# Load chunk sizes, fillers and the weights' gate, first weight products in halves of 256 columns, and output products moved into the first and split in the last block of an attention-and-MLP kernel

## The chip, the cores and the metric

The kernel runs on one core of one Trainium2 chip. The metric is the device time of one execution in microseconds (us). Beside it stands the span that the profiler records, from the first to the last instruction of one execution; it is some 1.8 us shorter. The mean granted TensorE clock of a run is 1.000, 0.999 or 0.998, and in traces with 0.998 there is one stretch of 3.4 us at half clock (0.5 x 3.41 / 756 = 0.0023). I call a run at 0.998 "clock lost". In traces at 0.999 half of that or less lies inside the span, and it comes after PE's last product, where it costs nothing; I count all runs at 0.999 as "clock kept".

The engines: PE multiplies (its weight loads are PEld), DVE is VectorE, ACT is ScalarE, POOL is GpSimd, SP issues DMAs.

## The reference

```python
# q, k, v: (4, 6080, 256); w_in (256, 2048); w_out (2048, 256)
qn = q / (norm(q, axis=1) + 1e-6);  kn = k / (norm(k, axis=1) + 1e-6)
s = kn.transpose(0, 2, 1) @ qn / tau          # 256 x 256 for each of 4 heads
a = softmax(s)
x = (v @ a).reshape(24320, 256)
out = gelu_tanh(x @ w_in) @ w_out
```

The contraction of `s` runs over all 6080 rows, so no output row can begin before all of q and k of its head is there.

## The kernel before

The kernel folds `a @ w_in` into one 256 x 2048 matrix `aw` for each head. A head's rows are then taken in blocks of 512. One block is 8 slots (`NP`); a slot is four hidden products `hp` of 512 columns (0.86 us), one Gelu of 1024 columns on ScalarE (1.02 us), and 8 of the 64 output products `yp` of the block before. Heads 1 to 3 do their attention in between. Only head 0's attention is exposed: the first 38 us load q and k in ten chunks and form the Gram matrix `G` and the column sums behind them. `keep_clock` issues products whose results nobody reads ("fillers"), so that PE's clock isn't lowered while PE waits for loads.

```python
    first_chunks = chunks_of([6, 6, 6, 6, 6, 6, 4, 3, 2, 2], 7)   # slots of 128 rows; 64 odd rows go with chunk 7
    fillers = [0, 0, 5, 5, 5, 5, 3, 2, 1, 0]
    ...
    for n, ch in enumerate(first_chunks):
        ...                                    # cast on DVE (L242), squares on ACT
        keep_clock(fillers[n])                 # L137
        for s, rows in slots_of(ch):
            gram(G, qkb, s, rows, ...)         # L141
        ...                                    # column sums, L153
        if n == n_chunks - 4:                  # the "gate": chunk 6 has landed
            nc.gpsimd.tensor_copy(gate[:, 0:1], st[0:1, 1, 0, 0:1])
    ...
    # GpSimd's DMA queue, in order, behind the gate:
    #   w_in in 4 parts, v of block 1, w_out in 2 halves, q/k of head 1 chunk 0, v of block 2
```

Then the softmax and the first part of `aw`:

```python
    nc.scalar.activation(r, cols[:, 0:4], AF.Sqrt)          # L320: starts when the last column sum is there
    norms(r); Gs = scaled(G, r); keep_clock(5); T = turned(Gs)
    ...                                                     # exponentials
    vT0 = ...; vps = ...                                    # 8 transposes of v block 0 on PE
    nc.scalar.activation(vT0, vps, AF.Copy)
    keep_clock(1)
    ...                                                     # ScalarE loads the Gelu table
    rsinv = row_sums(eT)
    ...
    ps0 = [aw_product(0, ic, pY, "y") for ic in range(2)]   # 4 products of 512 columns
    for lo in (0, 256):
        for ic in range(2):
            nc.vector.tensor_scalar_mul(aw[:, ic, lo : lo + 256], ps0[ic][:, lo : lo + 256], rsinv[:, ic : ic + 1])
    for ic in range(2):
        aw_part(eT, rsinv, aw, 1, ic)
    ...
```

The blocks, and the end:

```python
            for i in range(NP):
                ...                                         # hp, Gelu
                more_aw(1)
                if before is not None:
                    todo = [(s, fc) for s in range(len(before["rows"])) for fc in range(FC)]
                    for s, fc in todo[len(todo) * i // NP : len(todo) * (i + 1) // NP]:
                        y_part(before, s, fc, fc + 1)
    ...
    for s in range(4):                                      # the last block's own output
        y_part(before, s, 0, FC)
```

v of block n + 2 is turned by DMA transposes (SP, L294) from rows that GpSimd's queue fetched (L280).

## Time and profile before

| | before |
|---|---|
| time, median of 4 runs | 758.18 us (757.82 to 758.25) |
| span and clock of the profiled run | 756.4 us, 0.998 |
| last column sum ready (square root, L320, starts) | 38.27 us |
| from there to the start of the last group of hidden products | 705.33 us |
| from there to the end of the span | 12.79 us |

The last three rows add up to the span (38.27 + 705.33 + 12.79 = 756.39; the page rounds spans to 0.1, so ends are taken from the times in ns that the traces hold). I use this division into **front, middle and end**, because a timed median here moves by several tenths of a us, and a trace resolves hundredths.

The page's first part (busy us, share of the span, instructions) says that PE is the bound:

```profile
PE 738.3 (98%) x5248; PEld 504.5 (67%) x5248; DVE 278.2 (37%) x484; ACT 419.8 (56%) x411; POOL 70.7 (9%) x127
```

Of 756.4 us PE is idle for 18: 9.0 before its first product, 4.0 after its last, and 5.1 between, 4.6 of these while q and k load.

The chain in order of time (start, duration, what) has one more place that the change addresses, the only wait inside the blocks:

```profile
51.61 1.03 ACT g L540
...
52.68 1.02 PE hp L536 x4
```

PE waits there for a Gelu at the end of block 0, where it has no output products yet to do meanwhile.

### The profile page before, as it was taken

Reading aid. Unit: us, or ns where it says so; the run is one execution under the profiler, and the core shown is the slowest. Engines: PE = TensorE matmul, PEld = TensorE weight load, DVE = VectorE, ACT = ScalarE, POOL = GpSimd, SP = SyncE. Lnnn points to the kernel's source line nnn. Section 1 sums busy time; section 2 is a strip of 40 time slices with the busy share of each in tenths; the row PEclk is TensorE's granted clock in tenths of the full one; section 3 lists DMA queues with packets and bytes.
Section 4 is the critical chain, followed back from the end, with each engine's and each line's share of the span. In section 5 each row is a group of like instructions: output and inputs, shape, how many; then the busy total and the mean of one; then the engine's idle time right before and its main releaser. Section 6 shows DMA issues by size and latency. Waiting matters only on the chain.

```text
span 756.4 us, 12305 instructions
## 1 busy us (share of the span) xinstructions
PE 738.3 (98%) x5248; PEld 504.5 (67%) x5248; DVE 278.2 (37%) x484; ACT 419.8 (56%) x411; POOL 70.7 (9%) x127
## 2 busy tenths in 40 slices
PE   4899999999999999999999999999999999999997
PEld 3556666667666666666666666666767666666666
DVE  4644545454402555553421455454441011011011
ACT  5675555555465555555555555555546655555552
POOL 0321011001021011001031000100101000000000
PEclk9999999999999999999999999999999999999999
DMA  8999957225149778313549375621412633322111
GB/s 364 355 206 168 177 84 155 54 42 83 42 93 215 134 137 132 73 43 64 102 93 220 83 135 96 126 79 47 82 42 79 110 83 72 68 76 52 41 57 56
DMA packets 80599, 83.59 MB, mean 111 GB/s; under 512 B 55456, under 2 KB 60064, under 8 KB 80544
## 3 DMA queue, kind: packets, MB, share of 16 engines
q0 software_dynamic: 17648, 32.97, 26.5%
q1 hardware_dynamic: 62672, 48.98, 24.3%
q8 instruction: 41, 0.67, 0.4%
q10 hardware_dynamic: 224, 0.85, 0.3%
q14 instruction: 14, 0.11, 0.1%
HBM read 78.91 MB, written 24.90 MB: 137 GB/s over the span
## 4 chain that ended last, share of the span: by engine, by line
PE 95%; DMA 3%; ACT 1%; DVE 0%; SPq 0%; issue 0%; DVEq 0%; ACTq 0%
PE yp L463 44%; PE hp L536 43%; PE G L141 5%; DMA st<-in_k_dram 3%; PE ps L201 2%; PE cols L153 1%; ACT sqb L247 0%; PE idle L137 0%; PE T L179 0%; DVE qkb L242 0%; SPq L80 0%; ACT g L540 0%; PE ps L345 0%; PE vps L333 0%; DVE Gs L171 0%
## 5 line engine op out<-in xcount | busy, mean ns | idle before, releaser
L540 ACT ACTIVATE g<-hp 128x1024 bf16<-128x1024 f32 (+1 forms) x384 | 389.3, 1014 | 308.9 <-PE hp L536 308.9
L463 PE MATMUL yp<-wout_bf,g 128*128 128x256 bf16 x3040 | 393.3, 273 | 0.0
L536 PE MATMUL hp<-vT,aw 128*128 128x512 bf16 (+1 forms) x1536 | 390.5, 377 | 0.2 <-ACT g L540 0.2
L463 PEld LDWEIGHTS <-g 128*128 128x128 bf16 x3040 | 297.5, 98 | 112.9
L536 PEld LDWEIGHTS <-aw 128*128 128x128 bf16 x1536 | 150.0, 98 | 105.3 <-issue 1.1
L480 DVE COPY ysb<-yp 128x512 f32<-128x512 f32 (+1 forms) x95 | 64.9, 683 | 403.1 <-PE yp L463 395.1
L404 DVE TENSOR_TENSOR acc<-acc,sq 128x512 f32<-128x512 f32 (+1 forms) x141 | 97.6, 692 | 4.8
L141 PE MATMUL G<-qkb 128*128 128x256 bf16 (+1 forms) x384 | 70.7, 285 | 13.6 <-DVE qkb L242 13.6
L403 DVE TENSOR_TENSOR sq<-qkb 128x512 bf16<-128x512 bf16 (+1 forms) x141 | 58.9, 418 | 0.0
L141 PEld LDWEIGHTS <-qkb 128*128 128x128 bf16 (+1 forms) x384 | 38.2, 102 | 23.0 <-DVE qkb L242 15.6
L280 POOL DMA_DIRECT2D vb<-in_v_dram x47 | 25.5, 544 | 142.8 <-DMA vT<-vb 135.9
L210 DVE TENSOR_SCALAR aw<-ps,rsinv 128x512 bf16<-128x512 f32 x30 | 22.3, 750 | 25.6 <-PE ps L201 25.3
L80 POOL DMA_DIRECT2D qkb<-in_q_dram x24 | 13.0, 540 | 152.1 <-PE hp L536 83.0
L247 ACT ACTIVATE sqb<-st 128x3072 bf16<-128x3072 f32 (+3 forms) x9 | 20.4, 2286 | 11.2 <-DMA st<-in_k_dram 11.2
L242 DVE CAST qkb<-st 128x3072 bf16<-128x3072 f32 (+4 forms) x11 | 14.7, 1345 | 14.9 <-DMA st<-in_k_dram 14.9
L201 PE MATMUL ps<-win_bf,eT 128*128 128x512 bf16 x60 | 17.7, 379 | 0.0
L414 POOL TENSOR_TENSOR r<-r,half 128x4 f32<-128x4 f32 x3 | 3.1, 1041 | 141.5 <-DVE r L413 141.5
L80 POOL DMA_DIRECT2D qkb<-in_k_dram x24 | 13.1, 544 | 5.0 <-DMA qkb<-in_q_dram 2.2
L521 POOL COPY g<-gr 128x1024 bf16<-128x1024 bf16 x2 | 2.1, 1037 | 104.1 <-PE yp L463 104.1
L439 DVE RECIPROCAL den<-den 128x256 f32<-128x256 f32 x6 | 10.5, 1753 | 0.2
L549 POOL COPY gr<-g 128x1024 bf16<-128x1024 bf16 x2 | 2.1, 1034 | 87.6 <-ACT g L540 87.6
L137 PE MATMUL idle<-filler 128*128 128x512 bf16 x32 | 9.2, 408 | 0.0
(60 smaller groups left out, 81.0 us busy)
## 6 DMA issues: line engine op xcount, KB each, us to landing
out_dram<-ysb SPq DMA_DIRECT2D x44, 512.0 KB, 2.9
vb<-in_v_dram POOLq DMA_DIRECT2D x43, 256.0 KB, 8.5
qkb<-in_q_dram POOLq DMA_DIRECT2D x21, 384.0 KB, 6.2
qkb<-in_k_dram POOLq DMA_DIRECT2D x21, 384.0 KB, 8.3
st<-in_q_dram SPq DMA_DIRECT2D x6, 768.0 KB, 10.3
st<-in_k_dram SPq DMA_DIRECT2D x5, 768.0 KB, 11.8
vT<-vb SPq DMA_TRANSPOSE x184, 3.8
out_dram<-ysb SPq DMA_DIRECT2D x4, 384.0 KB, 4.2
```

Source lines behind the costliest of these rows:

```text
L80: engines[x].dma_start(out=dst[:, x, 0:size, :], in_=src[b, s0 * 128 : (s0 + size) * 128, :].rearrange("(p s) c -> p s c", s=size))
L141: nc.tensor.matmul(G[:, ic, :], lhsT=qk[:rows, 1, s, ic * 128 : ic * 128 + 128], rhs=qk[:rows, 0, s, :], start=first and ic == 0, stop=las ...
L201: nc.tensor.matmul(ps, lhsT=eT[:, jc, ic * 128 : ic * 128 + 128], rhs=win_bf[:, jc, fs * 512 : fs * 512 + 512], start=jc == 0, stop=jc == 1)
L210: nc.vector.tensor_scalar_mul(dst, ps, scale)
L247: nc.scalar.activation(sqb[:rows, :, lo:hi], st[:rows, :, lo:hi], AF.Square)
L280: nc.gpsimd.dma_start(out=t[:, 0:n, :], in_=v_rows[r0 : r0 + n * 128, :].rearrange("(p s) c -> p s c", s=n))
L403: nc.vector.tensor_mul(sq[:rows], flat, flat)
L404: nc.vector.tensor_add(acc[:rows], acc[:rows], sq[:rows])
L463: nc.tensor.matmul(yp[:rows, at, :], lhsT=g[:, fc, s * 128 : s * 128 + rows], rhs=wout_bf[:, fc, :], start=fc == 0, stop=fc == FC - 1)
L480: nc.vector.tensor_copy(ysb[:, s0 : s + 1, :], yp[:, 0 : s + 1 - s0, :])
L536: nc.tensor.matmul(hp[:, j, :cols], lhsT=aw[:, cc, fc * 128 : fc * 128 + 128], rhs=vT[:, cc, :cols], start=cc == 0, stop=cc == 1)
L540: nc.scalar.activation(g[:, 2 * i : 2 * i + 2, :cols], hp[:, :, :cols], AF.Gelu_apprx_tanh)
```

## The change

Four parts, all small against the span:

1. **Loads.** Other chunk sizes; the 64 odd rows come with chunk 2 instead of 7; three more fillers ahead of chunks 4 and 5, two more later; the weights' gate opens on chunk 7 instead of 6.
2. **Softmax to first hidden product.** T's transposes in an order that lets two of them start on half of `Gs`; v block 0 evacuated half by DVE, half by ACT; the filler ahead of the row sums gone; the first products of `aw` only 256 columns wide, so that the first hidden product needs less. The Gelu table is loaded after the first scalings.
3. **Block 0** does 12 of its own output products in its last three slots; block 1 then has 7 or 6 a slot instead of 8.
4. **The end.** The last slot's output in two halves of 128 columns, each with its own copy and transfer.

```diff
-    first_chunks = chunks_of([6, 6, 6, 6, 6, 6, 4, 3, 2, 2], 7)
+    first_chunks = chunks_of([6, 6, 5, 6, 6, 6, 4, 4, 2, 2], 2)
-    fillers = [0, 0, 5, 5, 5, 5, 3, 2, 1, 0]
+    fillers = [0, 0, 5, 5, 6, 7, 4, 3, 1, 0]
...
-        if n == n_chunks - 4:
+        if n == n_chunks - 3:
...
-        for jc in range(2):
-            for ic in range(2):
+        for ic in range(2):
+            for jc in range(2):
                 nc.tensor.matmul(T[:, jc, ...], ...)
...
-    nc.scalar.activation(vT0, vps, AF.Copy)
-    keep_clock(1)
+        if cc == 0:
+            nc.vector.tensor_copy(vT0[:, cc, :], vps)
+        else:
+            nc.scalar.activation(vT0[:, cc, :], vps, AF.Copy)
...
-    ps0 = [aw_product(0, ic, pY, "y") for ic in range(2)]
-    for lo in (0, 256): ...                   # four scalings on DVE
+    for lo, pool, tag in ((0, pY, "y"), (256, pA, "a")):
+        for ic in range(2):
+            ...                               # two products of 256 columns
+            if lo == 0 and ic == 1:
+                nc.scalar.activation(dst, ps[:, 0:256], AF.Copy, scale=scale)
+            else:
+                nc.vector.tensor_scalar_mul(dst, ps[:, 0:256], scale)
...
-                more_aw(1)
+                more_aw(2 if i == 0 else 1)
                 if before is not None:
+                    n = -(-len(before["todo"]) // (NP - i))
+                elif i >= NP - 3:
+                    n = 4
...
-    for s in range(4):
-        y_part(before, s, 0, FC)
+    ...                                       # slots 0 to 2 as before
+    for c0 in (0, 128):
+        ...                                   # 16 products of 128 columns
+        nc.vector.tensor_copy(ysb, yp)
+        for (lo, row), eng in zip(before["rests"], (nc.sync, nc.scalar)):
+            eng.dma_start(out=out[row : row + rest, c0 : c0 + 128], in_=ysb[lo : lo + rest])
```

More of the change, by code (lines that the diff above doesn't have):

```diff
@@ L329 @@
     vT0 = vts.tile([128, 2, 512], BF16, tag="vT", name="vT")
-    vps = pH.tile([128, 2, 512], FP32, tag="h", name="vps")
     for cc in range(2):
+        vps = pH.tile([128, 2, 512], FP32, tag="h", name="vps")[:, 0, :]
         for s in range(4):
-            nc.tensor.matmul(vps[:, cc, s * 128 : s * 128 + 128],
+            nc.tensor.matmul(vps[:, s * 128 : s * 128 + 128],
                              lhsT=v0[:, s, cc * 128 : cc * 128 + 128],
                              rhs=ident, is_transpose=True)
-    nc.scalar.activation(vT0, vps, AF.Copy)
@@ L337 @@
-    keep_clock(1)
-    nc.scalar.activation(dummy, ones_f, AF.Gelu_apprx_tanh)
+        if cc == 0:
+            nc.vector.tensor_copy(vT0[:, cc, :], vps)
+        else:
+            nc.scalar.activation(vT0[:, cc, :], vps, AF.Copy)
     rsinv = row_sums(eT)
     aw = awp.tile([128, 2, D], BF16, tag="aw", name="aw")
-    def aw_product(fs, ic, pool=pA, tag="a"):
-        ps = pool.tile([128, 512], FP32, tag=tag, name="ps")
-        for jc in range(2):
-            nc.tensor.matmul(
-                ps,
-                lhsT=eT[:, jc, ic * 128 : ic * 128 + 128],
-                rhs=win_bf[:, jc, fs * 512 : fs * 512 + 512],
-                start=jc == 0, stop=jc == 1)
-        return ps
@@ L352 @@
-    ps0 = [aw_product(0, ic, pY, "y") for ic in range(2)]
-    for lo in (0, 256):
-        for ic in range(2):
-            nc.vector.tensor_scalar_mul(aw[:, ic, lo : lo + 256], ps0[ic][:, lo : lo + 256],
-                                        rsinv[:, ic : ic + 1])
-    for ic in range(2):
-        aw_part(eT, rsinv, aw, 1, ic)
-    aw_left = [(2, 0, pY, "y"), (2, 1, pY, "y"), (3, 0, pA, "a"), (3, 1, pA, "a")]
+    for lo, pool, tag in ((0, pY, "y"), (256, pA, "a")):
+        for ic in range(2):
+            ps = pool.tile([128, 512], FP32, tag=tag, name="ps")
+            for jc in range(2):
+                nc.tensor.matmul(
+                    ps[:, 0:256],
+                    lhsT=eT[:, jc, ic * 128 : ic * 128 + 128],
+                    rhs=win_bf[:, jc, lo : lo + 256],
+                    start=jc == 0, stop=jc == 1)
+            dst, scale = aw[:, ic, lo : lo + 256], rsinv[:, ic : ic + 1]
+            if lo == 0 and ic == 1:
+                nc.scalar.activation(dst, ps[:, 0:256], AF.Copy, scale=scale)
+            else:
+                nc.vector.tensor_scalar_mul(dst, ps[:, 0:256], scale)
@@ L361, in more_aw @@
+    nc.scalar.activation(dummy, ones_f, AF.Gelu_apprx_tanh)
+    aw_left = [(fs, ic, *((pA, "a") if fs == 2 else (pY, "y"))) for fs in range(1, 4) for ic in range(2)]
     def more_aw(n):
@@ L487, in y_part @@
                 out=out[r0 : r0 + n * 128, :].rearrange("(p s) c -> p s c", s=n), in_=ysb[:, 0:n, :])
-        for (lo, row), eng in zip(st["rests"] if s >= n else [],
-                                  (nc.sync, nc.scalar if alone else nc.sync)):
-            eng.dma_start(out=out[row : row + rest, :], in_=ysb[lo : lo + rest, s, :])
+        for lo, row in st["rests"] if s >= n else []:
+            nc.sync.dma_start(out=out[row : row + rest, :], in_=ysb[lo : lo + rest, s, :])
     rest = N % 128
-    assert rest <= 64
+    assert rest == 64 and B % 2 == 0
     kept = None
@@ L530 @@
                     now["rows"] = now["rows"] + [rest]
+            now["todo"] = [(s, fc) for s in range(len(now["rows"])) for fc in range(FC)]
             for i in range(NP):
@@ L541 @@
                                      AF.Gelu_apprx_tanh)
-                more_aw(1)
+                more_aw(2 if i == 0 else 1)
                 if before is not None:
-                    todo = [(s, fc) for s in range(len(before["rows"])) for fc in range(FC)]
-                    for s, fc in todo[len(todo) * i // NP : len(todo) * (i + 1) // NP]:
-                        y_part(before, s, fc, fc + 1)
+                    n = -(-len(before["todo"]) // (NP - i))
+                elif i >= NP - 3:
+                    n = 4
+                else:
+                    n = 0
+                for s, fc in [(before or now)["todo"].pop(0) for _ in range(n)]:
+                    y_part(before or now, s, fc, fc + 1)
                 next(fill, None)
@@ L553 @@
         aw = aw_next
-    for s in range(4):
-        y_part(before, s, 0, FC)
+    s = len(before["rows"]) - 1
+    for x, fc in before["todo"]:
+        if x < s:
+            y_part(before, x, fc, fc + 1)
+    for c0 in (0, 128):
+        yp = pY.tile([128, 512], FP32, tag="y", name="yp")[:, 0:128]
+        for fc in range(FC):
+            nc.tensor.matmul(yp, lhsT=before["g"][:, fc, s * 128 : s * 128 + 128],
+                             rhs=wout_bf[:, fc, c0 : c0 + 128], start=fc == 0, stop=fc == FC - 1)
+        ysb = before["ysb"][:, s, c0 : c0 + 128]
+        nc.vector.tensor_copy(ysb, yp)
+        for (lo, row), eng in zip(before["rests"], (nc.sync, nc.scalar)):
+            eng.dma_start(out=out[row : row + rest, c0 : c0 + 128], in_=ysb[lo : lo + rest])
 _INS = ['q', 'k', 'v', 'tau', 'moe_w_in', 'moe_w_out']
```

## The prediction

> **What bounds the kernel now.** I read three views of the profile of before: the table of stretches (it shows where which engine is full), the chain that ended last in order of time, and the timeline of the first 53 us and the last 15 us.
>
> The stretches first. The columns are us, then busy us of PE, its weight loads, VectorE, ScalarE and GpSimd (with instruction counts), the granted clock, the DMA share and GB/s.
>
> ```profile
> 18.50:22.20 3.70, 3.20 (x35) 2.02 (x32) 2.54 (x3) 2.68 (x2) 0.00 (x0) 1.00 1.03 420
> 22.20:27.30 5.10, 3.72 (x33) 2.07 (x31) 2.58 (x2) 2.73 (x1) 0.00 (x0) 1.00 1.01 405
> 27.30:29.80 2.50, 0.66 (x6) 0.61 (x7) 2.48 (x2) 2.47 (x1) 0.00 (x0) 0.98 1.01 392
> 29.80:32.00 2.20, 2.20 (x22) 1.46 (x21) 2.18 (x3) 2.10 (x2) 2.15 (x4) 0.50 1.06 311
> ...
> 53.00:100.00 47.00, 47.00 (x334) 32.32 (x332) 21.36 (x40) 25.48 (x26) 5.41 (x11) 1.00 0.89 156
> ```
>
> From 53 us to 744 us PE is busy 47.00 of 47.00 us and the change leaves that work alone: its 256-column products run at 7.88 us / 72 = 109 ns, its 512-column ones at 0.86 us / 4 = 215 ns. So of 758 us only two pieces can move: the first 53 us and the last 12. In the first, the loads of q and k fill the DMA engines (share 1.01 to 1.03, about 420 GB/s) until some 29 us. Then comes what the row 29.80:32.00 shows: PE is busy throughout, but at a clock of 0.50, after a row in which it worked 0.66 of 2.50 us. Steps of half a microsecond put the slow clock from 29.68 to 33.09 us. The chain shows that PE, not the load, then sets the end:
>
> ```profile
> 27.32 1.77 DVE qkb L242
> 29.09 0.05 issue
> 29.14 2.25 PE G L141 x12
> 31.39 0.30 PE cols L153 x12
> 31.68 1.30 PE idle L137 x3
> ...
> 36.65 0.32 PE idle L137
> ...
> 40.44 0.87 PE vps L333 x8
> 41.31 0.21 PE idle L137
> 41.53 0.08 PE rs L188 x4
> ```
>
> The sixth chunk (number 5) lands at 27.27 us, its products begin at 29.14 us, and PE never pauses again before 38.24 us, when the last column sum ends. The last chunk landed at 35.46 us, so PE was 2.8 us behind it. On that path lie six filler products (line 137, no useful work): 3 for 1.30 us, 2 for 0.45 us, 1 for 0.32 us, together 2.07 us.
>
> **What the Trainium skill says.** "TensorE: Matmul & The Clock Gate", section "What's actually happening": the clock is halved after an idle window, the windows are 3413 ns long and run freely, not from the kernel's start. The trace agrees: 29.68 to 33.09 us is 3.41 us. Counting back, the window that caused it is 26.27 to 29.68 us: PE stopped at 26.84 and began at 29.13, idle 2.29 of 3.41 us. The window before it had 0.92 us idle and lost nothing. The same page, "Back-to-back issue gap", gives N / 2.4 GHz + 2.5 ns warm: 56, 109, 216 ns for 128, 256, 512 columns; the trace has 0.45 us / 8 = 56 ns, 109 and 215. "ScalarE: Activation LUTs", "What ACT_TABLE_LOAD costs": 1283 ns a load plus a drain of about 1380 ns. The trace has 1283 ns but no drain: the Gelu load at 42.39 us is followed by its dummy at 43.68. "DMA: Bandwidth & Descriptors", "Queues, rings and completion order": a DMA engine takes turns between queues, packet by packet, so weight loads begun early slow the q and k loads. The trace agrees: with the first weight issues at 29.97 us the row falls from 392 to 311 GB/s.
>
> **The change, part by part.**
>
> 1) Chunk sizes, fillers, gate. The odd rows (64 of them) move from chunk 7 to chunk 2 and chunk 2 loses a slot, so chunks 0 to 5 are 35.5 slots and not 36. A slot of q and k is 0.262 MB; half of one at 0.42 MB/us is 0.31 us. Chunk 5 lands at 27.27 - 0.31 = 26.95. Up to chunk 7 the bytes are the same, 43.5 slots. The weight loads now wait for chunk 7, not 6 (29.84 us), so chunks 7 to 9 no longer share the engines: 4 + 2 + 2 slots at about 0.41 MB/us after chunk 6 (29.5) land at 32.0, 33.3, 34.55 us. That is 0.9 us earlier than 35.46.
> PE: fillers ahead of chunk 5 are 7, not 5. Chunk 4's products end 0.31 us earlier, at 25.1; column sums end at 25.35; seven fillers at 0.216 plus a tail end near 26.95. Chunk 5's products start at 26.95 + 1.8 = 28.75. The gap falls from 2.29 to 1.8 us, at most 53% of a window (it was 67%). If that keeps the clock full, PE runs from 28.75: G 12 products 1.48 (as at 20.19 us in the timeline), sums 0.44, 4 fillers 0.86, G 8 0.98, sums 0.44 + 0.54, 3 fillers 0.65, G 8 0.98, sums 0.54, filler 0.22, G 0.44, sums 0.2, G 0.45, sums 0.2: total 8.42, end at 37.2 us. Before it was 38.24: **-1.05 us**. Two more fillers on the path cost 0.43 of it. If the clock is lost again, those 3.41 us do half the work; I put in 1.5 us (the same 12 G products took 2.25, the 3 fillers 1.30: 0.77 + 0.65 too much by those two groups alone). Then the end is 38.7: +0.45 us.
>
> 2) From the last sum to the first hidden product. Before: sum end 38.24, transposes end 40.44 (first 0.30, then 3 in 0.55), exponentials 40.48 to 41.32, row sums at 41.53 because eight transposes of v (0.87) and a filler (0.21) stood ahead. Now two transposes need only the first half of Gs, so all four end near 40.26 (0.18 less), and the filler is gone: row sums at 41.18. **-0.35 us**.
> Then 8 products of 256 columns (0.87) instead of 4 of 512 (0.86). The first hidden product needs two scaled halves. Before they were two VectorE instructions in turn, 480 ns each, done at 42.95, hidden under four more products of PE until 43.36. Now PE has only its 0.87 + 0.08 us, to 42.13 on before's clock. VectorE evacuates half of v (a 512-wide copy, 0.69) from about 40.9, so the reciprocal comes at 41.6 to 41.8, then one scaling on each engine to 42.3. PE waits about **+0.2 us**. The six remaining products (2.6 us) only move behind hidden ones, so PE's total is unchanged. ScalarE: exponentials end 41.14, v half and scaling (about 0.5 each) to 42.3, table 1.28, dummy 0.2: first Gelu at about 43.8 against 44.25. The second Gelu's product is ready later than that, so nothing waits on it.
>
> 3) Output products of block 0 in its last slots: 12 move from block 1 to block 0, 12 x 109 ns = 1.3 us, no work removed. Worth only PE's idle there, which the timeline shows once (0.23 us at 52.68, waiting for Gelu): **-0.23 us**. ScalarE needs 1.02 us a slot and PE alone 0.86, so only this lets PE stay ahead.
>
> 4) The end.
>
> ```profile
> 744.52 7.88 PE yp L463 x72
> 752.39 0.02 issue
> 752.41 0.42 DVE ysb L484
> ```
>
> The last slot becomes two halves of 128 columns: 32 x 56 ns = 1.79 us for 16 x 109 = 1.74 (+0.05). The last copy is 128 wide: 512 take 0.69 and 256 take 0.42, so I estimate 0.29 (-0.13). The last transfer (2.2 us to landing) is half as large but mostly fixed. **-0.1 us**.
>
> Sum with the clock kept: -1.05 - 0.35 + 0.2 - 0.23 - 0.1 = **-1.5 us: 756.65**. With the clock lost: +0.45 - 0.48 = 0: **758.1**.
>
> **The rivals.** (a) The clock is lost in spite of the fillers: a gap of 1.8 us remains, and 2.29 was too long while 0.92 was not; where the window falls is chance. 758.1 us, one in three. (b) The weights arrive late, since their gate opens at 32.0 and not 29.8. Before, GpSimd's own waits show the four w_in parts landing near 38.1, 39.3, 40.6 and 42.3, w_out near 46.2 and 48.6. The DMA engines stay full in either kernel, so the sum of bytes ends as before; the first part is needed at 40.2 now, the w_out halves near 49 and 51.6. Margins of 1 to 3 us; if all shifted by the full 2.2 us, the first would cost 0.1 to 0.3 us. Small either way. (c) The q and k loads stay the bound: 34.55 plus cast, square and sums (1.4 us) is 36.0, below PE's 37.2. So PE bounds, and fewer fillers would gain more. (d) The loads lose more: only eight transfers of one queue are in flight, and the odd rows now take two of them early, so chunk 3 is issued at 7.1 instead of 3.2. With chunks 1 and 2 (3 MB, 7 us) queued, engines don't run dry: 0.
>
> **Range and chances.** Two in three for 756.65, one in three for 758.1; middle pulled a little up: **756.9 us**, range 755.8 to 758.3 (below: chunk 5 is not late at all and the gap closes; above: clock lost and some weight late). Two per cent is 15 us, ten times the sum of all terms: faster 0.005, same 0.99, slower 0.005.
>
> **What would show it.** Stretches: clock 1.00 at 29.8 to 33 means step 1 holds; 0.50 means rival (a). Chain: last column sum at 37.2; row sums 2.95 us after it; first hidden product 1.1 us later, with a small wait on VectorE or ScalarE; no wait for Gelu in block 0; the last copy about 0.3 us. PE waiting on a w_in or w_out transfer would mean rival (b). I am wrong if the time before 53 us shrinks by over 2.5 us or grows.

## The result, and the profile after

After: 757.4 us median of 4 runs (757.1 to 757.9), against 758.18. The ratio is 0.9991, with a 95% interval of 0.9974 to 1.0009. The class is "same". Three of the four runs kept the clock, the fourth (757.9 us) lost it.

| | before | after | difference |
|---|---|---|---|
| span of the profiled run, clock | 756.4, 0.998 | 755.3, 1.000 | -1.1 |
| front: last column sum ready | 38.27 | 37.19 | -1.08 |
| middle: to the start of the last hidden group | 705.33 | 705.74 | **+0.41** |
| end | 12.79 | 12.40 | -0.39 |

PE's totals on the page hardly move: 24 more instructions, 0.3 us less busy.

```profile
PE 738.0 (98%) x5272; PEld 504.6 (67%) x5272; DVE 278.3 (37%) x485; ACT 420.3 (56%) x412; POOL 70.0 (9%) x127
```

The stretches of after, with the columns of the prediction's first fence (busy us of PE, its weight loads, DVE, ACT and POOL, then granted clock, DMA share, GB/s):

```profile
29.80:32.00 2.20, 2.20 (x28) 1.62 (x26) 2.20 (x3) 2.20 (x2) 0.00 (x0) 1.00 1.02 388
53.00:100.00 47.00, 46.62 (x327) 31.66 (x326) 22.58 (x43) 26.18 (x26) 7.00 (x14) 1.00 1.01 171
```

First row: the clock is 1.00 where before had 0.50, 28 products instead of 22, and no POOL work, because the gate is still shut. Second row: PE was full in before (47.00 of 47.00 us); now 0.38 us are missing. That was not predicted.

The chain of after, through the front and to the place where the 0.38 us are:

```profile
27.60 1.77 DVE qkb L242
29.42 1.48 PE G L141 x12
31.18 0.89 PE idle L137 x4
...
36.85 0.31 PE cols L153 x8
...
40.44 0.23 PE rs L188 x3
...
41.56 1.00 PE hp L536 x4
...
64.89 0.88 PE hp L536 x4
...
65.79 1.03 ACT g L540
...
67.00 1.02 PE hp L536 x4
```

The last sum ends at 37.16 (36.85 + 0.31), the row sums begin at 40.44, the first hidden product at 41.56. The wait in block 0 is gone, but a wait of the same kind now stands at 67.00, at the start of block 2. The chain puts it down to a Gelu; e1 and e5 show that it is not one.

The end of after, in the same view:

```profile
743.85 6.11 PE yp L463 x56
749.96 1.80 PE yp L567 x32
...
751.79 0.29 DVE ysb L570
```

56 products of 256 columns and 32 of 128 take 7.91 us (before: 72 in 7.88), and the last copy 0.29 us (before 0.42).

### The profile page after: what moved, and what is told of

Its sections match the earlier page's. It is cut to its first block, busy times and chain, and to the rows that moved or that the text cites. A ratio compares the mean times of both kernels' runs of the same rounds, so it can differ in the third digit from the quotient of the medians. Undisturbed runs are those within 1.5% of the kernel's fastest.

```text
span 755.3 us, 12358 instructions
## 1 busy us (share of the span) xinstructions
PE 738.0 (98%) x5272; PEld 504.6 (67%) x5272; DVE 278.3 (37%) x485; ACT 420.3 (56%) x412; POOL 70.0 (9%) x127
## 4 chain that ended last, share of the span: by engine, by line
PE 95%; DMA 3%; DVE 0%; ACT 0%; SPq 0%; issue 0%; DVEq 0%
PE yp L463 44%; PE hp L536 44%; PE G L141 5%; DMA st<-in_k_dram 3%; PE ps L201 2%; PE cols L153 1%; PE T L179 0%; PE yp L567 0%; PE idle L137 0%; SPq L80 0%; DVE qkb L242 0%; ACT g L540 0%; PE ps L348 0%; ACT eT L328 0%; DVE Gs L171 0%
## 5 line engine op out<-in xcount | busy, mean ns | idle before, releaser
L80 POOL DMA_DIRECT2D qkb<-in_k_dram x24 | 13.1, 544 | 4.1 <-DMA qkb<-in_q_dram 2.3
```

The costliest lines, as they stand in the source:

```text
L80: engines[x].dma_start(out=dst[:, x, 0:size, :], in_=src[b, s0 * 128 : (s0 + size) * 128, :].rearrange("(p s) c -> p s c", s=size))
```

## The experiments

The question after the result: which part gives which of the three differences, and why did the middle grow by 0.41 us when parts 2 and 3 should have shrunk it? My theory was the gate: opened on chunk 7, it makes everything in GpSimd's queue late, and the queue also carries what block 2 needs. One rival was the order in that queue (v of block 2 stands behind q and k of head 1). Another was that the moved products themselves make the stall. On the front the question was whether the fillers, the sizes or the gate bring the 1.08 us. The comparison with the reference passed for all (e11 feeds wrong data for 64 of 6080 rows of head 0, and still fell within the tolerance).

| run | from | edit | median us (runs) | ratio to before, 95% | span, clock | front + middle + end |
|---|---|---|---|---|---|---|
| e1 | after | gate back on chunk 6 | 757.09 (5) | 0.9984 [0.9972, 0.9997] | 754.6, 1.000 | 37.20 + 704.96 + 12.40 |
| e2 | after | v of block 2 asked for first | 758.02 (5) | 0.9998 [0.9984, 1.0012] | 756.2, 0.998 | 38.44 + 705.40 + 12.40 |
| e3 | after | 5 and 5 fillers | 757.62 (5) | 0.9993 [0.9980, 1.0005] | 755.2, 1.000 | 36.97 + 705.86 + 12.38 |
| e4 | before | 6 and 7 fillers | 758.05 (5) | 0.9997 [0.9985, 1.0010] | 756.3, 0.999 | 38.22 + 705.33 + 12.78 |
| e5 | before | all of part 1 | 758.22 (4) | 1.0002 [0.9987, 1.0017] | 756.1, 1.000 | 37.23 + 706.10 + 12.80 |
| e6 | e1 | no early output products | 758.0 (4) | 0.9998 [0.9984, 1.0011] | 757.0, 0.998 | 39.21 + 705.36 + 12.40 |
| e7 | e1 | end whole, as in before | 756.91 (4) | 0.9985 [0.9971, 0.9999] | 755.3, 1.000 | 37.52 + 704.95 + 12.79 |
| e8 | e1 | softmax part as in before | 756.98 (4) | 0.9991 [0.9976, 1.0006] | 754.8, 1.000 | 37.45 + 704.93 + 12.40 |
| e9 | after | head 1's q and k asked for later | 757.62 (5) | 0.9998 [0.9986, 1.0011] | 755.8, 0.998 | 38.50 + 704.96 + 12.38 |
| e10 | e1 | 12 fillers ahead of chunk 5 | 756.54 (6) | 0.9981 [0.9969, 0.9994] | 754.6, 1.000 | 37.22 + 704.95 + 12.38 |
| e11 | after | odd rows not loaded | 756.4 (one look) | none | 754.6, 0.999 | 36.26 + 705.85 + 12.51 |
| e12 | e10 | gate on chunk 5 | 759.02 (4) | 1.0015 [1.0001, 1.0029] | 758.2, 0.998 | 40.05 + 705.78 + 12.38 |

Before itself ran at 758.26 in the first call (9 runs; e1 to e4), 758.17 in the second (9; e6 to e9) and 758.15 in the third (10, of which nine are those of the second; e5, e10 to e12). The intervals are about 2 us wide, so of the timed comparisons only e1, e7, e10 and e12 are told from before at all. No interval between two variants was worked out. What follows about tenths of a us rests on the traces.

### e1: the gate back on chunk 6

```diff
-        if n == n_chunks - 3:
+        if n == n_chunks - 4:
```

> The changed kernel with the weight loads gated on chunk 6 again, as before the change. Theory A (the PE wait of 0.38 us at 67.0 us comes from the gate: the software queue runs 2 us late, so the v rows of block 2 land at 55 instead of 53 us and their transposes end late): that wait is gone, the transposes are issued near 53 us, DVE's first step of the norms is back from 0.42 to about 0.17 us (it collides with GpSimd writing the w_out transfer), while chunks 7 to 9 land some 0.5 us later; net -0.7 to 0.2 us against the changed kernel's 757.4. Theory B (the wait is Gelu's, made by the new order of output products): the wait at the start of block 2 stays, and the time is worse by what the loads lose, 0.3 to 0.8 us.

Measured: 757.09 us; the span falls by 0.77 to 754.56. In this pair of traces the loads are no slower: DVE begins to cast the last chunk at 35.34 us (after: 35.44), the front is 37.20 against 37.19. But fronts scatter more than middles do. e7, e8 and e10 also have these sizes, the gate on chunk 6 and the clock kept; over the four the last cast begins at 35.34 to 35.68 and the front is 37.20 to 37.52, against 36.97 to 37.23 in the three traces with the gate on chunk 7 and the clock kept (after, e5, and e3 with its fewer fillers). So the earlier gate may cost the front some 0.2 us (the difference of the two means); these runs do not settle it. The middle is 704.93 to 704.96 in all four.

The middle falls from 705.74 to 704.96, by 0.78. Two places in the trace account for it. The first is the first step of the norms on DVE, a 128 x 4 instruction. In the timeline of after, with the first of the two issues of w_out on POOL above it (a window that leaves out the second):

```profile
36.92 0.91 POOL L313 DMA_DIRECT2D wout_bf<-in_moe_w_out_dram  x1
37.40 0.42 DVE L164 TENSOR_SCALAR r<-r 128x4 f32<-128x4 f32 x1 [0.65 <-ACT r L320]
```

and in the timeline of e1, with the Gelu and the hidden products around 66 us:

```profile
37.41 0.17 DVE L164 TENSOR_SCALAR r<-r 128x4 f32<-128x4 f32 x1 [0.65 <-ACT r L320]
...
65.55 1.02 ACT L540 ACTIVATE g<-hp 128x1024 bf16<-128x1024 f32 x1 [0.49 <-PE hp L536]
...
66.22 1.03 PE L536 MATMUL hp<-vT,aw 128*128 128x512 bf16 x4
```

The same instruction takes 0.42 us in after, where it starts inside the first w_out issue (36.92 to 37.83) and ends at 37.82, and 0.17 us in e1, where both are issued by 36.68. Over all traces: 0.42 to 0.44 in after, e3, e5 and e11, which have the gate on chunk 7 and the last sum by 37.23 us, and in each of the four it ends 0.01 us or less before that issue does; 0.17 in the ten others, which have an earlier gate or, with the clock lost, a later sum. So it looks as if the step waits for the issue. Not every issue does this: in e2 the step lies inside an issue of v (38.51 to 39.10 us), in e9 inside one of q, and takes 0.17. What in the issue holds it up is not shown. The step lies on the path, so 0.25 us are lost there. The second is block 2's first group, straight on other products in e1, and in after behind 0.38 us of idle and 0.16 slower (1.02 instead of 0.86): 0.54 us. Together 0.79, against 0.78 measured. (In the timeline each group of four lasts 1.03 us, because it counts the end of the last product, which overlaps the next group; the chain counts each moment once, so it has 0.86 for a group in a row and 1.02 for one after a wait.)

The e1 fence also answers whether that wait is for the Gelu: here the Gelu of block 1's last slot runs until 66.57, and block 2's first hidden products already begin at 66.22. So they don't need it.

### e2: v of block 2 ahead of q and k of head 1

```diff
-    load_qk(1, 0)
-    load_v(2)
+    load_v(2)
+    load_qk(1, 0)
```

> The changed kernel with the v rows of block 2 asked for ahead of the first q and k chunk of the next head; nothing else moves. Theory A (late v rows of block 2): their transposes are issued at 51 to 52.5 us instead of 55.1, PE does not wait at the start of block 2, time 0.4 to 0.6 us below the changed kernel, 756.9. Theory B (Gelu makes that wait): wait and time unchanged within 0.1 us.

A miss, and instructive. The rows of v came 3.2 us earlier: SP issued the first transpose at 51.94 us instead of 55.15. But the fourth transpose, the last that block 2 needs, landed at 67.67, later than in after (66.75), and the stall stayed (0.29 us idle and the slower group). So rows of v that land earlier are not enough: the four transposes took 9 to 13 us from issue to landing.

What moves with the fourth transpose in all 14 traces is another transfer, the last one that GpSimd's queue then has under way: the k half of a chunk of head 1, issued at 52 to 55 us. The transpose lands 0.6 to 1.2 us after that k, never before it: k at 65.79 and the transpose at 66.75 in after, 64.14 and 65.36 in before, 63.66 and 64.62 in e1. e2 put q and k back, so k was issued at 55.25 instead of 54.57 and landed at 67.09. That fits e2's miss, and it is the theory C that e9 was to test; it is seen in the traces, not shown by a run that moves k alone.

In four of e2's five runs the clock was lost (the profiled one too: slow from 29.47 to 32.89 us, after a gap of 1.98 us), which is why its front is 38.44; more on that in e3.

### e3 and e4: fillers alone

e3 takes the added fillers ahead of chunks 4 and 5 out of after; e4 puts them into before.

```diff
# e3, against after
-    fillers = [0, 0, 5, 5, 6, 7, 4, 3, 1, 0]
+    fillers = [0, 0, 5, 5, 5, 5, 4, 3, 1, 0]
# e4, against before
-    fillers = [0, 0, 5, 5, 5, 5, 3, 2, 1, 0]
+    fillers = [0, 0, 5, 5, 6, 7, 3, 2, 1, 0]
```

> The changed kernel with 5 and 5 fillers ahead of chunks 4 and 5 instead of 6 and 7. If the extra fillers keep the clock (step 1): PE's gap before chunk 5 grows from 1.9 to 2.4 us, the clock falls to 0.50 for 3.4 us from about 29.7 us, the last column sum moves from 37.16 to 38.2 to 38.7 us, time up by 0.6 to 1.5 us. Rival (the chunk sizes keep it, the fillers do nothing): clock 1.00, time within 0.2 us of the changed kernel.

> The kernel before with 6 and 7 fillers ahead of chunks 4 and 5, its late fillers (3, 2, 1), sizes and gate kept. If the clock alone is the gain of step 1: clock 1.00 at 29.7 to 33 us, the last column sum at 36.9 to 37.3 instead of 38.24, time 0.9 to 1.3 us below before (756.9 to 757.3), so as good as the whole change. Rival (sizes and gate matter): the clock holds but the sum ends after 37.6 us because PE waits for chunks slowed by the weights, gain under 0.6 us.

e3: PE's gap ahead of chunk 5 grew back to 2.31 us (1.94 in after). The profiled run kept the clock all the same, but three of its five runs lost it. Before, with a gap of 2.29 us, lost it in 13 of 19 runs. The eight kernels with the new sizes and 7 fillers (after, e1, e2, e5 to e9) lost it in 11 of 35. With e4 below (added fillers on before: lost in 1 of 5) the counts suggest that the fillers change the chance; five runs of a kernel don't prove it, and a single profile doesn't show it.

e4: four of five runs kept the clock (0.999; in the traced one it was slow only after PE's last product), and yet nothing was gained: front 38.22 against 38.27. PE worked off its backlog and then stood waiting for the load, as this line of e4's timeline shows (in brackets the idle time before it, and its releaser):

```profile
37.27 0.61 PE L141 MATMUL G<-qkb 128*128 128x256 bf16 x4 [0.76 <-DVE qkb L242]
```

The last chunk was cast from 36.39 us on, 0.9 later than in before (35.46). Fillers alone are worth nothing in before, by this trace and by the times (758.05 against 758.26). That load is 0.9 us later behind a stretch in which the transfers fell to 152 to 195 GB/s (30 to 31.5 us). The weights are not the reason: no packet of their queue moves before 33.43 us in e4 (33.03 in before), over 3 us after the gate has opened. What does move there is the odd rows, which come with chunk 7 in before and e4: their packets of 1 KB run from 29.3 to 32.5 us in e4, from 29.5 to 32.0 in before. In after they run from 13.1 to 13.7, and there the rate falls too (e11). Why it cost more in e4 than in before is open.

### e5: part 1 alone, on before

```diff
# against before: chunk sizes, fillers and gate of after; nothing else
```

> The kernel before with step 1 alone: new chunk sizes, fillers and gate on chunk 7. If the clock holds: last column sum near 37.2 us instead of 38.24, but the weight queue starts 2.7 us later, so the DMA backlog ends later and PE waits at the start of block 2 (0.3 to 0.6 us), and DVE's first norm step takes 0.42 us. Expected: span 0.3 to 0.6 us below before. If instead the loads behind the gate cost nothing, the whole 1.05 us of the prediction should show in the span.

Front 37.23: nearly the whole gain of after's front, 1.03 us. Middle 706.10: 0.77 us given back. All four runs kept the clock, and the median is still 758.22, no better than before. e5 has no moved output products and yet stalls, and e1 has them and does not, so they do not make the stall. In e5 the chain follows it back to the gate:

```profile
32.77 0.17 POOL gate L261
32.94 2.76 POOL win_bf L309 x3
35.70 8.18 DMA win_bf<-in_moe_w_in_dram
...
44.17 11.01 DMA vb<-in_v_dram
...
55.19 1.33 SPq L294
...
59.65 7.51 DMA vT<-vb
...
67.40 0.38 PE hp L536
```

Read from the bottom: block 2's hidden product at 67.40 waited for a transpose of v that landed at 67.16; the transposes were issued when the rows of v had landed at 55.17; GpSimd asked for those 0.28 us after a part of w_in had landed at 43.88 (in the traces of before, after and e5 at most eight of its transfers are under way at a time); and w_in was asked for when the gate opened at 32.77. e3's chain has the same links. A chain names at each step what came last; that v landed late is one of its links, but e2 shows that this link alone does not set the end. The name in after's chain, "ACT g", was a coincidence of 0.06 us: the Gelu ended at 66.81, the fourth transpose landed at 66.75, and PE began at 67.00. From the landing to PE it is 0.25 us in e5, e3, e2 and after alike, while the Gelu ends 0.37 us before PE begins in e5 and 0.30 before in e3.

The margin makes the size plain. In before PE would begin block 2 at 67.83, and the fourth transpose had landed at 65.36: 2.5 us to spare. In after PE would be there 1.2 us earlier (about 66.6), and the transpose lands 1.39 us later (66.75). Both movements are the change's own. In e1 it landed at 64.62 and PE came at 66.22.

### e6, e7, e8: parts 3, 4 and 2, each undone on e1

They are built on e1, where the gate's price in the middle is gone.

```diff
# e6, against e1
-                elif i >= NP - 3:
-                    n = 4
# e7, against e1: the end of before (lines that go are left out)
...
+    for s in range(4):
+        y_part(before, s, 0, FC)
# e8, against e1: order of T's transposes, one evacuation of v on ACT, the filler,
#                 first products 512 wide with four scalings on DVE, more_aw(1)
```

> Base: the changed kernel with its gate on chunk 6, which had no PE wait at the start of block 2. Here the output products of block 0 stay in block 1, as before the change. My step 3: PE waits for Gelu once in block 0 again, 0.23 us idle plus 0.16 us of a slower first group, so block 2's first hidden product stands about 0.4 us further from the last column sum than in the base (29.2 us there); time +0.4 us. Rival: it is hidden, because in the base PE reaches block 0's last slots later relative to Gelu; distance within 0.1 us.

> Same base, with the last slot of the output in one piece of 256 columns as before the change. My reading of the two traces: PE's end to the last copy's end grows from 0.31 to 0.44 us, PE's part shrinks by 0.05, and the time from the last copy to the span's end grows from 3.2 to 3.55 us: together the span from the last hidden product's start is about 0.4 us longer. Rival (the first estimate, 0.1 us, and the rest was chance): 0.1 us.

> Same base, with the code between the norms and the first hidden product as before the change (one evacuation of v on ScalarE, one filler, 512-column first products, transposes in the old order). My step 2 said 0.35 us earlier row sums and 0.2 us lost before the first hidden product. In the base the row sums start 3.02 us after the last column sum; expected here 3.29 us as in the kernel before, and no wait of PE on a scaled half (0.14 us); block 2's first hidden product 0.1 to 0.3 us further from the last sum than in the base. Rival (part 2 is worth nothing): within 0.05 us.

e6: the middle grows by 0.40 (705.36 against 704.96), and the wait of before is back at its place in the chain:

```profile
51.68 0.88 PE hp L536 x4
...
52.58 1.03 ACT g L540
...
53.66 1.02 PE hp L536 x4
```

The next group starts when the Gelu has ended, and has 1.02 us instead of 0.86. e6's profiled run lost the clock, so its front (39.21) is no measure of the part.

e7: the end grows by 0.40 (12.793 against 12.398). Over all traces the end is 12.78 to 12.80 us in the four kernels with a whole last slot (before, e4, e5, e7) and 12.38 to 12.51 in the ten with two halves. The copy explains 0.13 of it, as this line of e7's timeline shows against the 0.29 us of after:

```profile
751.28 0.42 DVE L484 COPY ysb<-yp 128x256 f32<-128x256 f32 x1 [1.32 <-PE yp L463]
```

The rest is the time from the end of the last copy to the end of the span: 3.55 us in e7 and before, 3.25 in e1 and after. Of these 0.30 us, 0.17 are the last transfer, 2.07 us from issue to landing in e1 and 2.24 in e7. The other 0.13 come after its landing (1.15 us to the end of the span instead of 1.28), and no run explains them: e11 has two halves and 1.28. The timed median of e7 (756.91) doesn't show a loss against e1 (757.09); at intervals this wide it couldn't.

e8: the middle is 704.93 with the old softmax part and 704.96 with the new one. Part 2 is worth nothing. The chains of both say why. The row sums begin 3.02 us after the last sum in e1 and 3.29 in e8: 0.27 won, as intended. From there to the end of the first weight products it is 1.12 us in e1 (40.20 to 41.32) and 0.96 in e8 (40.72 to 41.68): 0.16 lost. And e1's first hidden group has 1.00 us instead of 0.86, because nothing stands between it and the scaled halves that it needs: 0.14 lost. The first hidden product does start earlier, 4.14 us after the last sum instead of 5.12, but PE is no further with its work, and PE is the bound.

### e9: an edit that moved nothing

```diff
-            load_qk(b, n + 2)
             qk = loaded_of.pop((b, n))
             for s, rows in slots_of(ch):
+                if s == min(3, ch[1] - 1):
+                    load_qk(b, n + 2)
```

> The changed kernel, gate on chunk 7 as it is, but the q and k chunk after next is asked for three slots later (about 60 us instead of 54 us for the first one), so less is queued ahead of the v transposes of block 2. New theory C (PE's wait at 67 us ends when the whole backlog of the DMA engines has drained, wherever v stands in the queue): those transposes land before 65 us instead of 66.8, no PE wait at the start of block 2, time 0.3 to 0.6 us below the changed kernel at the same clock. Rival (it is the order of v in the software queue alone): the transposes still land at 66.5 to 67 us.

A miss of my own making. It was to test whether q and k of head 1, in flight from 54 us on, hold up the transposes. GpSimd takes its queue in order, and the transfer in question was issued at 54.14 us, in after at 54.05. So e9 is after once more, this time with the clock lost in the profiled run (slow from 29.85 us, after a gap of 1.94, as long as the one in after that lost nothing), and the question stays open. It shows one thing all the same. With the clock lost the front ends 1.31 us later than in after, but PE begins block 2 only 0.68 us later (67.68 against 67.00): a later PE meets transposes that have landed (67.09). A slip in the front and a slip in the queue don't add up.

### e10: more fillers

```diff
# against e1
-    fillers = [0, 0, 5, 5, 6, 7, 4, 3, 1, 0]
+    fillers = [0, 0, 5, 5, 6, 12, 4, 3, 1, 0]
```

> Meant as the best version: the changed kernel with its gate on chunk 6 and 12 fillers, not 7, ahead of chunk 5, which fill PE's wait for that chunk to within 1 us. If the clock depends on the length of that gap: clock kept (1.000, or 0.999 with a dip after the last product) in all runs, last column sum at 37.0 to 37.4 us, no PE wait at the start of block 2, median 756.3 to 757.0. If the gap is not what decides, some runs show 0.998 again and the median stays near 757.1.

The gap ahead of chunk 5 falls to 0.93 us, as e10's timeline shows (the first line is the fillers):

```profile
25.66 2.75 PE L137 MATMUL idle<-filler 128*128 128x512 bf16 x12
29.34 1.37 PE L141 MATMUL G<-qkb 128*128 128x256 bf16 x11 [0.93 <-DVE qkb L242]
```

Five more fillers cost nothing, because PE would have waited there: the chunk's products begin at 29.34 (29.42 in after), and front, middle and end are those of e1 to 0.02 us. All six runs kept the clock. At the rate of the kernels with 7 fillers (24 of 35 kept) that would happen by chance in one case in ten, 0.69 to the sixth; so it is likely, not proven, that the fillers did it. The median of 756.54 us is the lowest of the kernels with right results, 1.6 us below before and 0.9 below after; against after that rests on different calls.

### e11: what the odd rows cost

```diff
# against after, head 0 only
-                engines[x].dma_start(out=dst[:REM, x, size, :], in_=src[b, S_ALL * 128 : N, :])
+            nc.gpsimd.memset(dst[:REM, :, size, :], 0.01)
```

> Wrong result on purpose: the changed kernel without the two transfers of the 64 odd rows of the first head (a constant is put there). They are 0.13 MB, 0.31 us of the load at 0.42 MB/us. If they cost only their bytes: chunk 9 lands 0.3 us earlier, 35.1 us. If their small packets or an uneven share of the engines make the load end late (the rate fell to about 300 GB/s for 2 us around them, and the engines were 0.4 busy in the last microsecond of the load): 0.6 to 0.9 us earlier, 34.5 to 34.8. If the instruction fetch at 24 to 26 us alone makes the tail uneven, the engines are again half idle for a microsecond before chunk 9 lands.

Chunk 5 was cast at 26.64 us instead of 27.60, the last chunk at 34.51 instead of 35.44: 0.93 to 0.96 us for two transfers of 64 rows of 1 KB, 0.13 MB together. At the 0.42 MB/us of the other loads they would take 0.31. The stretch 13 to 15 us shows the rate, in e11

```profile
13.00:15.00 2.00, 2.00 (x11) 1.40 (x10) 1.47 (x2) 1.60 (x2) 0.00 (x0) 1.00 1.02 416
```

and in after, with the same DMA share of over 1.0 but fewer bytes:

```profile
13.00:15.00 2.00, 2.00 (x11) 1.44 (x10) 1.26 (x2) 1.40 (x2) 0.00 (x0) 1.00 1.04 306
```

This is a size, not a mechanism: why small rows cost three times their bytes no run here isolates, nor whether part of it is the two places that they take among the eight loads under way. The span is 0.71 below after's, less than the 0.93: the middle is 0.11 longer (PE comes earlier and waits 0.46 us at block 2 instead of 0.38), the end 0.11.

### e12: the gate one chunk earlier still

```diff
# against e10: gate on chunk 5
-        if n == n_chunks - 4:
+        if n == n_chunks - 5:
```

> As the best version, with the weight loads gated on chunk 5 (27.4 us), one chunk earlier still. If q and k share the engines evenly with the weights, chunk 9 lands 0.5 to 1 us later and the last sum with it: 0.3 to 0.8 us slower than with chunk 6. If the load's end is set by its own tail, as the equal landings with gates on chunks 6 and 7 suggest (35.34 and 35.44), the time is within 0.2 us of it.

The slowest kernel, 759.02 us. In its chain the last chunk's load takes the front:

```profile
28.30 9.86 DMA st<-in_k_dram
...
38.28 0.70 DVE qkb L242
```

The last chunk is cast from 38.28 us on, 2.9 later than in e10 (35.38). When it has landed, GpSimd's queue has moved 0.63 MB, against 0.18 in e10. So weights do take time from q and k if the gate opens while four chunks are still under way. With the gate on chunk 6 they take 0.2 us or so, if anything (e1). Of the three places tried chunk 6 is the best. The 0.83 us more in the middle is the clock, slow here from 39.32 to 42.73 us after a gap of 1.86; the two runs that kept it took 758.74 and 758.80 us, still more than any run of e10.

## Why the prediction was right or wrong

The number was right: 757.4 for 756.9, inside the range, and "same". The sum behind it was right only because errors in its terms cancelled in part: the end and block 0 gave more than was reckoned, part 2 gave less, and the gate cost more.

- **Bound.** Right. PE is full between the front and the end in every kernel, but for the one wait in block 0 or at block 2.
- **Step 1, "-1.05 us".** Measured -1.08 (after) and -1.03 (e5), with the clock kept. But two mistakes cancelled, which is luck. The last sum was to end at 37.2 and ended at 37.16; yet chunk 5's products were to start at 28.75 and started at 29.42, and PE's work from there was to take 8.42 us and took 7.74. The start was late because the odd rows cost 0.93 us of load time where I had reckoned them by their bytes (e11). The work was shorter because I had read its pieces too long, the sums from the timeline, where they overlap: the chain of after has 0.28, 0.68 and 0.38 for the sums (0.44, 0.98 and 0.54 in my list) and 0.87 for eight products (0.98). And the step "chunks 7 to 9 no longer share the engines", worth 0.9 us, was false: the last chunk was cast at 35.44 (before 35.46), and with the gate back on chunk 6 at 35.34 to 35.68. It rested on a misreading. The fall from 392 to 311 GB/s in before is not the weights, of which no packet moves before 33.03 us, but goes with the odd rows (e4); with the same gate and the odd rows elsewhere e1 has 388 in that row.
- **The clock, "one in three".** 11 of 35 runs of the kernels with these sizes and fillers. The price was put at 1.5 us; in the traces that lost it (e2, e9) the front ended 1.25 and 1.31 us later than in after (e6: 2.01 later than in e1, of which 0.74 is a later chunk 5), and by e9 part of that is absorbed at block 2.
- **Step 2, "-0.35 us" and "+0.2 us".** Measured 0.0 (e8 against e1). The row sums were to come 2.95 us after the last sum; they came after 3.28 in after and 3.02 in e1. The difference of 0.25 is the slowed DVE step. Even in e1 the saving was 0.27, and the wait put at 0.2 was 0.30 (0.16 + 0.14): it took all of the gain.
- **Step 3, "-0.23 us".** Measured -0.40 (e6 against e1). Mechanism right, term too small: I counted the idle time and not that the first group after an idle time takes 0.16 us longer.
- **Step 4, "-0.1 us".** Measured -0.39 (after) and -0.40 (e7 against e1). The products (+0.03) and the copy (-0.13) are as worked out. The last transfer is "mostly fixed", 2.07 us instead of 2.24, but the 0.17 were left out of the sum; so were 0.13 after its landing, whose cause stays open.
- **Rival (b), "Small either way".** This is the step that failed most. I looked for its price at the first use of w_in and w_out, "0.1 to 0.3 us". It was 0.78 us, and at neither of them: 0.25 at a DVE step on the path that now falls beside an issue of w_out, and 0.54 at block 2, whose transposes land only when the transfers behind the weights in GpSimd's queue have landed. I followed the delayed transfers to their own readers and not to the transfers behind them. (The landings were also read 0.3 to 0.6 us too late, from waits that end that long after them: w_in landed at 37.83 to 41.97, w_out at 45.69 and 48.35.)
- **Rival (c)** was nearly right: chunk 9 bounded closer than I thought. Its cast began at 35.44, 1.7 us before PE's end, where I had reckoned with 34.55.

Sum of what was measured with the gate's price apart: -1.06 (front, e1) - 0.38 (middle) - 0.39 (end) = -1.83 us, e1's span against before's. The gate on chunk 7 takes 0.77 of that away. The timed medians show -0.8 for after and -1.6 for e10.

**Still open:** why the transposes land only after the last transfer that GpSimd's queue has under way (so in all 14 traces, but e9 moved nothing and no other run tried it), what holds the DVE step beside the issue of w_out, and why the odd rows cost three times their bytes.

## What to carry to other kernels

When an issue queue is held back by a gate, follow everything that stands behind the gate to its reader, also what is read 30 us later and what other queues have under way beside it, and note the margin of each; before opening a gate later, look in the trace whether the packets it holds back move at all while the loads it protects are under way. Where a wait's name in the chain rests on an event some hundredths of a us from another, look at a variant in which the two fall apart, as e1 and e5 did here. Where a view merges two instructions into one line, ask for a window that parts them, as for the issues of w_out. Fillers in a place where the engine waits anyhow are free, and their effect on the clock is a matter of chances: count it over runs, not in one profile.

## What the Trainium skill lacked or had wrong

- "TensorE: Matmul & The Clock Gate", section "HAM oscillation — how this bites in real kernels", gives as its rule "no PE-idle gaps >~3.4µs". Here gaps of 2.29 us (before), 1.98 (e2), 1.94 (e9) and 1.86 (e12) were followed by 3.41 us at half clock, 0.67 to 0.55 of 3.41 us; 1.94 us in after was not, nor 2.31 in e3's profile. So below a full window the length of the gap alone does not decide, and the page has no figure for that range; with a gap of 0.93 us ahead of chunk 5 (e10) none of six runs lost it.
- "SBUF — State Buffer", section "SBUF: two separate sides", says that of a DVE and a GpSimd operation that need the shared port pair one blocks the other for the whole of its instruction. The 128 x 4 DVE step beside the first w_out issue fits that: 0.42 us instead of 0.17, ending at 37.82, and the issue at 37.83. The page does not say for which part of a DMA issue GpSimd holds the pair: inside an issue of v (e2) or of q (e9) the same step took 0.17. That the pair is the cause is not shown by these runs.
- No page has a figure for how long a DMA transpose waits beside transfers of another queue. Here the fourth transpose of block 2 landed 0.6 to 1.2 us after the last transfer that GpSimd's queue had under way, in all 14 traces, 7 to 12 us after its own issue.
